# A convolution head that needs only half of its weights to start: one copy on every second partition, the second copy behind

## The chip, the cores and the metric

One core of a Trainium2 chip. The metric is the device time of one execution in microseconds. The kernel before took 275.3 us, the median of 3 runs (274.16 to 279.05).

## What is computed

A 7x7 convolution of a 224x224 image with 96 channels in and out, circular in both directions, written in the reference with FFTs:

```
x: (1, 224, 224, 96) bf16      w: (7, 7, 96, 96) bf16
wp = pad(w, to 224 x 224 in the first two axes)
Xf = rfft2(x over H, W);  Wf = rfft2(wp over H, W)
Yf = einsum('bhwi,hwio->bhwo', Xf, Wf)
y  = irfft2(Yf, (224, 224)).astype(bf16)
```

## The kernel before, in words

**Tiling.** Along H the image is cut into 8 blocks of 28 rows (`NJ`, `B`), and each is transformed with its 6 halo rows by a DFT of length 34: 17 frequencies `s` of two real values. Along W nothing is transformed: the 7 taps are applied directly, two columns at a time. Along W the image is cut into 7 tiles `t` of 32 columns.

**Forward transform.** For each column a matmul of 118 image rows (`xn`, for tile 0 `x0_bufs` at the end of `WF`) by the matrix `Fm` gives the channels on the partitions (`xf`). `f_jobs(t, part)` makes such jobs for a part of the frequencies; `jg` 0 and 1 are the upper and lower four blocks. A job is some 5 to 8 matmuls into one PSUM bank and one cast to `xf`. `jit` then forms sums and differences of `xf` (`J`, called planes here) on VectorE for three frequencies at a time.

**Weights.** `wqx` holds the 49 taps. Before, each tap has two partitions: row 2k holds the tap's 96x96 matrix from its start, row 2k+1 the same from half of the output channels on (`C2` elements later). So one matmul with a strided stationary operand (128 input channels, a step of 96 elements) and the matrix `Em` as the moving one gives two output channels, k and k + 48, for all slots of a group of frequencies. `Em` has a half for the even and a half for the odd rows, with zeros in the others' place. `prep_jobs(gi)` makes 12 jobs of 4 such matmuls for a group of `PGRP`; group 0 is frequencies 0 and 1 (5 slots of 10 taps), the others three frequencies each, for which `diff` forms a third slot per frequency as a difference on VectorE. The results go to `WF`.

**Rounds.** `b_round(t, s)` convolves one frequency of one tile: a first bank, a fill (`mid`), a second bank, a fill (`end`). Fills are jobs of the lists `qs`, with a first and a last fill number each (`add(a, b, jobs)`; round r has fills 2r and 2r + 1), handed out evenly by `pace`. A difference of frequency s must come before round s. Tiles 0 and 1 run interleaved, tile 1 four rounds behind; the others follow one by one.

**Order.** Every engine runs its instructions in program order (`_Ordered`), and so does the queue of transfers on SyncE. Which of VectorE and ScalarE casts a bank is chosen when the program is made, by `evac` with costs of 180 + 1.0n and 160 + 0.85n ns and the running sums `load`.

**The head.** Lines 184 to 190 issue the loads: halo columns, tile 0's pixels of `jg` 0, the weights in two transfers (96 rows, then the last tap's 2 rows), tile 0's pixels of `jg` 1. `warm` (lines 196 to 201) keeps TensorE busy with dummy matmuls on `wu`. Line 222 zeros the end of `wqx`. Lines 683 to 700 are the order of TensorE's work: halo, the forward jobs of `jg` 0, three times nine dummy matmuls, the weights of group 0, the forward jobs of `jg` 1, then tile 1's pixels are requested, planes, rounds.

Of the kernel before, what the change touches and what calls it, by code (L numbers as in the profile page):

```python
# [9 lines left out]
F32 = mybir.dt.float32  # L10
# [15 lines left out]
NB = 8  # L26
POS = TW + HALO
NTAP = 10
TAPS = ((7, 8, 9, 6), (0, 2, 4, 6), (1, 3, 5))
NSLOT = 2 + 3 * (NS - 1)  # L30
PGRP = ((0, 2), (2, 5), (5, 8), (8, 11), (11, 14), (14, 17))
# [16 lines left out]
def slot(s, part):  # L48
    return part if s == 0 else 2 + 3 * (s - 1) + part
# [3 lines left out]
def kernel(  # L53
# [7 lines left out]
    _, H, W, C = x.shape  # L61
# [5 lines left out]
    PW = KT * KT  # L67
    FR = 2 * NS
    PW2 = 2 * PW
    C2 = C // 2  # L70
# [37 lines left out]
    def bank():  # L108
        return pools["psb"].tile([128, 512], F32, name="pb")
# [28 lines left out]
    def dma(out_ap, in_ap):  # L138
        return DE.dma_start(out=out_ap, in_=in_ap)

    WF = cpool.tile([128, NSLOT, NTAP, C], BF16, name="WF")
# [17 lines left out]
    stmp = stmp_cm.__enter__()  # L159
    wqx = wtmp.tile([128, C - 1 + 127 * C + 1], BF16, name="wq")  # L160
    wq = wqx[0:PW2]
    WC = C * C - C2
    Em = wqx[0:PW2, WC:WC + 2 * NSLOT * NTAP].rearrange("p (h a t) -> p h a t", h=2, a=NSLOT)
    XHW = PAD * C + 32
    late = WF[0:R, NSLOT - 8:NSLOT].rearrange("p a t o -> p (a t o)")
    x0_bufs = [late[:, i * (XW + 32):(i + 1) * (XW + 32)] for i in range(2)]
# [14 lines left out]
    def load_x(t, jg):  # L181
        return load_rows(xbuf(t, jg), jg, t * 2 * TW, 2 * TW)
# [2 lines left out]
    for jg in range(2):  # L185
        load_rows(xh_bufs[jg], jg, W - PAD, PAD)
    load_x(0, 0)
    for k, n in ((0, PW - 1), (PW - 1, 1)):
        dma(wqx[2 * k:2 * (k + n), 0:WC], bass.AP(wsrc.tensor, wsrc.offset + k * C * C, [[C * C, n], [C2, 2], [1, WC]]))
    load_x(0, 1)  # L190

    wu = cpool.tile([128, 128], BF16, name="wu")
    wur = wu[:].unsqueeze(1).to_broadcast([128, 4, 128])
# [2 lines left out]
    def warm(n):  # L196
        pwu = bank()
        for _ in range(n):
            TE.matmul(pwu[:].rearrange("p (a b) -> p a b", a=4), lhsT=wu[:, 0:128], rhs=wur, start=True, stop=True)
    warm(8)  # L200
    warm(9)

    ntmp = [0]

# [13 lines left out]
    VE.memset(pi_t[:], math.pi)  # L218
    dmy = ftile([128, 1])
    SE.activation(out=dmy[:], in_=pi_t[:], func=ACTF.Sin, bias=0.0, scale=0.0)  # L220
    zw = wqx[0:PW2, WC + 2 * NSLOT * NTAP:]
    SE.copy(out=zw, in_=wu[0:PW2, 0:1].to_broadcast(list(zw.shape)))

    nrj = ftile([R, JG]); pw_i = ftile([R, 1]); aa = ftile([R, NS, 2]); phf = ftile([R, NS, 2]); phe = ftile([R, NS, 2])
    twc = ftile([PW2, KT]); mf = ftile([R, JG, NS * 2])
# [19 lines left out]
    floor_div(VE, fl[:], qq[:], Q)  # L245
    VE.scalar_tensor_tensor(out=qq[:], in0=fl[:], scalar=-float(Q), in1=qq[:], op0=ALU.mult, op1=ALU.add)
    SE.activation(out=qq[:], in_=qq[:], func=ACTF.Sin, bias=pi_t[:R, :], scale=-2.0 * math.pi / Q)

    GE.memset(mf[:], 1.0)
    GE.affine_select(out=mf[:], in_=mf[:], pattern=[[-B, JG], [0, NS * 2]], compare_op=ALU.is_ge, fill=0.0, base=0, channel_multiplier=1)  # L250
# [26 lines left out]
    VE.tensor_single_scalar(out=pv[:, :, 0], in_=qe[:, 1:, 0], scalar=-2.0, op=ALU.mult)  # L277
    VE.tensor_tensor(out=pv[:, :, 1], in0=qe[:, 1:, 1], in1=qe[:, 1:, 0], op=ALU.subtract)
    VE.tensor_tensor(out=pv[:, :, 2], in0=pv[:, :, 0], in1=pv[:, :, 1], op=ALU.subtract)
    for k0, k1 in ((0, slot(PGRP[0][1], 0)), (slot(PGRP[0][1], 0), NSLOT)):  # L280
        VE.tensor_tensor(out=Em[:, :, k0:k1], in0=pe3[:, k0:k1].unsqueeze(1).unsqueeze(3).to_broadcast([PW2, 2, k1 - k0, NTAP]),
                         in1=mk2[:].unsqueeze(2).to_broadcast([PW2, 2, k1 - k0, NTAP]), op=ALU.mult)

    def build_g(nj):
        PG = nj * FR

        def floor_g(out_ap, in_ap, d):
            GE.tensor_scalar(out=out_ap, in0=in_ap, scalar1=1.0 / d, scalar2=-(d - 1) / (2.0 * d), op0=ALU.mult, op1=ALU.add)
            GE.tensor_single_scalar(out=out_ap, in_=out_ap, scalar=MAGIC, op=ALU.add)
            GE.tensor_single_scalar(out=out_ap, in_=out_ap, scalar=MAGIC, op=ALU.subtract)  # L290

        def mod_g(out_ap, in_ap, fl_ap, d):
            floor_g(fl_ap, in_ap, d)
            GE.tensor_single_scalar(out=out_ap, in_=fl_ap, scalar=-float(d), op=ALU.mult)
            GE.tensor_tensor(out=out_ap, in0=out_ap, in1=in_ap, op=ALU.add)
        p = ftile([PG, 1]); sp = ftile([PG, 1]); rm = ftile([PG, 1]); jp = ftile([PG, 1]); rr = ftile([PG, 1]); z = ftile([PG, 1])
        iota(p[:], [[0, 1]], cm=1)
        mod_g(rm[:], p[:], jp[:], FR)
        mod_g(rr[:], rm[:], sp[:], 2)
        GE.tensor_single_scalar(out=z[:], in_=sp[:], scalar=0.0, op=ALU.is_equal)  # L300
        zr = ftile([PG, 1]); ag = ftile([PG, 1]); pg = ftile([PG, 1]); amp = ftile([PG, 1]); pgt = ftile([PG, 1])
        GE.tensor_tensor(out=zr[:], in0=z[:], in1=rr[:], op=ALU.mult)
        GE.tensor_scalar(out=ag[:], in0=zr[:], scalar1=17.0, scalar2=sp[:, 0:1], op0=ALU.mult, op1=ALU.add)
        GE.tensor_single_scalar(out=ag[:], in_=ag[:], scalar=2.0, op=ALU.mult)
        GE.tensor_tensor(out=pgt[:], in0=rr[:], in1=zr[:], op=ALU.subtract)
        GE.tensor_scalar(out=pg[:], in0=pgt[:], scalar1=17.0, scalar2=17.0, op0=ALU.mult, op1=ALU.add)
        GE.tensor_scalar(out=amp[:], in0=z[:], scalar1=-1.0 / L, scalar2=2.0 / L, op0=ALU.mult, op1=ALU.add)
        nm = ftile([PG, nj, B]); jc = ftile([PG, nj, B]); msk = ftile([PG, nj, B]); fl = ftile([PG, nj, B]); th = ftile([PG, nj, B])
        iota(nm[:], [[0, nj], [1, B]], base=PAD)
        iota(jc[:], [[1, nj], [0, B]])  # L310
        GE.tensor_scalar(out=msk[:], in0=jc[:], scalar1=jp[:, 0:1], scalar2=amp[:, 0:1], op0=ALU.is_equal, op1=ALU.mult)
        GE.tensor_scalar(out=nm[:], in0=nm[:], scalar1=ag[:, 0:1], scalar2=pg[:, 0:1], op0=ALU.mult, op1=ALU.add)
        mod_g(th[:], nm[:], fl[:], Q)

        def fin():
            SE.activation(out=th[:], in_=th[:], func=ACTF.Sin, bias=pi_t[0:PG, :], scale=-2.0 * math.pi / Q)
            GE.tensor_tensor(out=G.rearrange("p (j m) -> p j m", j=nj), in0=th[:], in1=msk[:], op=ALU.mult)
        return fin

    g_fin = build_g(3)  # L320

    def prep_jobs(gi):
        s0, s1 = PGRP[gi]
# [364 lines left out]
    for p in range(2):  # L688
        for f in fj[p][0]:
            f()  # L690
    for _ in range(3):
        warm(9)
    for f in prep_jobs(0)[0]:
        f()
    last = [f() for f in fj[0][1]]
    for jg in range(2):
        for d in load_x(1, jg):
            tc.add_manual_dep(d.ins, last[0].ins.name, SYNC, reason="second tile's pixels later")
    for f in jit(0, 0):
        f()  # L700
    g_fin()
    stmp_cm.__exit__(None, None, None)
    yf_pool = ctx.enter_context(tc.tile_pool(name="yf", bufs=YBUF))
# [21 lines left out]
    def add(a, b, jobs):  # L725
        qs.append([a, b, jobs, len(jobs)])

    for gi in range(1, len(PGRP)):
        pj, dj = prep_jobs(gi)
        add(2 * PGRP[gi - 1][0], 2 * PGRP[gi - 1][1] - 1, pj)  # L730
        for i, f in enumerate(dj):
            k = 2 * (PGRP[gi][0] + i) - 2
            add(k, k + 1, [f])
    for t in range(2):
        scr_tiles[t] = dr_pool.tile([TW, NJ, NS, 4 * C], BF16, name="scr")
# [9 lines left out]
    for r in range(NS + LAG):  # L745
        if r == 0:
            add(0, 4, fj[1][1])
        for p in range(2):
            if r == (1, 3)[p]:
                new_xf(1, SH2[1][p], SH2[1][p + 1])  # L750
                fj = f_jobs(1, p)
                if p == 1:
                    for jg in range(2):
                        fj[jg][-1] = then_load(fj[jg][-1], 2, jg)
                add(2 * r + 1, 2 * r + (5, 8)[p], fj[0] + fj[1])
        for p in range(3):
            if r == (9, 14, 17)[p]:
                new_xf(2, SH2[2][p], SH2[2][p + 1])
                fj = f_jobs(2, p)
                if p == 2:  # L760
                    for jg in range(2):
                        fj[jg][-1] = then_load(fj[jg][-1], 3, jg)
                add(2 * r, 2 * r + (8, 7, 5)[p], fj[0] + fj[1])
        if r == PGRP[-2][1] + 1:
            assert not any(q[2] for q in qs[:4 * len(PGRP) - 8])
            wtmp_cm.__exit__(None, None, None)
            t_pool = ctx.enter_context(tc.tile_pool(name="tt", bufs=NTT, side="right"))
            t2_pool = ctx.enter_context(tc.tile_pool(name="tt2", bufs=1, side="right"))
            yo_pool = ctx.enter_context(tc.tile_pool(name="yo", bufs=2, side="right"))
            g_pool = ctx.enter_context(tc.tile_pool(name="gp", bufs=1, side="right"))  # L770
            GA = g_pool.tile([KA, 4 * B], BF16, name="GA")
            GB = g_pool.tile([128, 2, 4 * B], BF16, name="GB")
            GE.memset(GA[:], 0.0)
            GE.memset(GB[:], 0.0)
        if r == NS + 3:
            queue_c(0)
        for t in range(2):
            s = r - LAG * t
            if not 0 <= s < NS:
                continue  # L780
            now = bursts.pop((r, t), ())
            now = jit(*now) if now else ()
            both = LAG <= r < NS
            b_round(t, s, fills(qs, 2 * r + (t if both else 0)), fills(qs, 2 * r + (t if both else 1)), False, now)
# [116 lines left out]
```

## Time and profile before

| what | value |
|---|---|
| median of 3 runs | 275.3 us |
| span in the profile | 275.8 us |
| TensorE busy | 260.8 us |
| VectorE, ScalarE busy | 227.8, 196.3 us |
| DMA moved | 46.79 MB, mean 170 GB/s |
| granted TensorE clock over the span | 0.993 |
| transfer of the weights (96 rows) | 1719 KB |

How to read it: all instructions go through one helper, so each has line L87, and groups are told apart by the names of their tiles: `pb<-wq` is a weight matmul, `pb<-Fm,xn` or `pb<-Fm,WF` a forward one (tile 0's pixels lie in `WF`), `pb<-WF,xf` and `pb<-WF,J` the convolution, `pb<-wu` a dummy. PE is a matmul, PEld the load of its stationary operand. Times in the stretches and in the timeline are microseconds from the start of the span. In the timeline the first number is the start, the second how long the merged group lasted, and square brackets hold idle time before it and what ended it.

### The profile page before, as it was taken

How to read it: one execution, taken by the hardware profiler on the slowest of the kernel's cores; microseconds unless marked ns; L12 is line 12 of the kernel's file. 1: busy time of each engine (PE TensorE's matmuls, PEld its weight loads, DVE VectorE, ACT ScalarE, POOL GpSimd, SP SyncE). 2: the span in 40 equal slices, each digit the busy share in tenths (PEclk: the TensorE clock that was granted, in tenths of full speed). 3: DMA queues.
4: the chain of work that ended last, by engine and by line, in shares of the span. 5: the costliest groups of instructions: out<-in, count | busy, mean ns of one | idle time of the engine just before them, and what ended most of it. 6: DMA issues, size and time to landing. Idle time of an engine off the chain costs nothing.

```text
span 275.8 us, 12056 instructions
## 1 busy us (share of the span) xinstructions
PE 260.8 (95%) x5088; PEld 238.9 (87%) x5088; DVE 227.8 (83%) x469; ACT 196.3 (71%) x475; POOL 102.2 (37%) x152
## 2 busy tenths in 40 slices
PE   8969999989998999999999999999999999999972
PEld 3649998989998999899999999999999999999751
DVE  5528999998999889977976897788988889899933
ACT  5518997768774566898988869888887874653522
POOL 7720033445446455233243215222432242654200
PEclk9988999999999999999999999999999999999999
DMA  6954313411111189787979487977949833979775
GB/s 176 239 99 128 88 48 108 146 50 48 45 60 67 55 243 191 198 244 230 315 211 256 131 239 222 220 200 200 295 132 180 275 124 110 206 213 241 185 185 181
DMA packets 46211, 46.79 MB, mean 170 GB/s; under 512 B 35274, under 2 KB 37846, under 8 KB 46058
## 3 DMA queue, kind: packets, MB, share of 16 engines
q1 hardware_dynamic: 45692, 44.34, 59.3%
q0 software_dynamic: 464, 1.67, 1.8%
q8 instruction: 40, 0.66, 1.1%
q14 instruction: 15, 0.12, 0.1%
HBM read 24.65 MB, written 21.33 MB: 167 GB/s over the span
## 4 chain that ended last, share of the span: by engine, by line
PE 56%; DVE 17%; DMA 12%; issue 6%; ACT 4%; POOL 3%; SPq 2%; DVEq 0%
PE pb L87 56%; DVE J L87 6%; DMA wq<-in_w_dram 5%; DMA tt<-scr 5%; DVE WF L87 4%; DVE v L87 3%; POOL yf L87 3%; DVE u L87 2%; SPq L87 2%; ACT xf L87 2%; DMA xf<-scrl 2%; ACT WF L87 1%; DVE yf L87 1%; DVE yo L87 0%; DVE xf L87 0%
## 5 line engine op out<-in xcount | busy, mean ns | idle before, releaser
L87 PE MATMUL pb<-WF,J 96*128 96x96 bf16 x2898 | 167.6, 206 | 1.4 <-DVE J L87 0.6
L87 PEld LDWEIGHTS <-J 96*128 96x128 bf16 x2898 | 141.5, 98 | 10.7 <-DVE J L87 1.7
L87 POOL TENSOR_TENSOR yf<-v,u 128x384 bf16<-128x384 f32 x85 | 85.2, 1018 | 141.7 <-issue 84.8
L87 ACT CAST xf<-pb 96x408 bf16<-96x408 f32 (+5 forms) x142 | 66.9, 492 | 7.8 <-PE pb L87 5.8
L87 PE MATMUL pb<-WF,xf 96*128 96x96 bf16 x952 | 61.0, 206 | 2.9 <-DVE WF L87 2.1
L87 DVE TENSOR_TENSOR J<-xf 96x1824 bf16<-96x1824 bf16 (+1 forms) x84 | 60.3, 756 | 0.1
L87 PEld LDWEIGHTS <-xf 96*128 96x128 bf16 x952 | 47.4, 98 | 3.8 <-issue 3.1
L87 PE MATMUL pb<-Fm,xn 118*128 118x136 bf16 (+4 forms) x576 | 44.5, 203 | 0.0
L87 ACT CAST WF<-pb 96x480 bf16<-96x480 f32 (+1 forms) x60 | 30.0, 561 | 8.4 <-PE pb L87 8.1
L87 PE MATMUL pb<-tt,Gm 102*84 102x384 bf16 (+1 forms) x132 | 33.6, 327 | 0.0
L87 PEld LDWEIGHTS <-xn 118*128 118x128 bf16 x576 | 29.2, 98 | 0.1
L87 ACT CAST yo<-pb 84x384 bf16<-84x384 f32 (+1 forms) x61 | 26.3, 480 | 4.1 <-PE pb L87 4.0
L87 ACT CAST J<-pb 84x384 bf16<-84x384 f32 (+1 forms) x62 | 26.8, 482 | 2.7 <-PE pb L87 2.7
L87 DVE TENSOR_TENSOR J<-J 96x912 bf16<-96x912 bf16 (+1 forms) x42 | 24.9, 594 | 0.0
L87 PE MATMUL pb<-wq 98*128 98x120 bf16 (+1 forms) x288 | 22.9, 234 | 2.1 <-DMA wq<-in_w_dram 2.1
L87 PEld LDWEIGHTS <-wq 98*128 98x128 bf16 x288 | 20.5, 151 | 2.5 <-issue 2.5
L87 PE MATMUL pb<-wu 128*128 128x512 bf16 (+3 forms) x70 | 18.7, 398 | 1.1 <-DVE ct L87 1.1
L87 DVE TENSOR_TENSOR yf<-v,u 128x384 bf16<-128x384 f32 x27 | 15.6, 578 | 0.9
L87 DVE TENSOR_TENSOR WF<-WF 96x960 bf16<-96x960 bf16 x15 | 15.8, 1057 | 0.2
L87 PEld LDWEIGHTS <-wu 128*128 128x128 bf16 (+3 forms) x70 | 7.9, 115 | 8.4 <-issue 2.9
L87 DVE CAST WF<-pb 96x400 bf16<-96x400 f32 (+1 forms) x12 | 7.2, 608 | 8.4 <-PE pb L87 8.1
L87 PEld LDWEIGHTS <-Gm 102*84 102x84 bf16 (+1 forms) x132 | 11.5, 117 | 1.7 <-issue 0.6
(394 smaller groups left out, 236.9 us busy)
## 6 DMA issues: line engine op xcount, KB each, us to landing
scr<-yf SPq DMA_DIRECT2D x30, 288.0 KB
xn<-in_x_dram SPq DMA_DIRECT2D x12, 672.0 KB
tt<-scr SPq DMA_DIRECT2D x24, 336.0 KB
out_dram<-yo SPq DMA_DIRECT2D x12, 252.0 KB
out_dram<-J SPq DMA_DIRECT2D x12, 252.0 KB
tt<-scr SPq DMA_DIRECT2D x6, 288.0 KB
wq<-in_w_dram SPq DMA_DIRECT2D x1, 1719.0 KB
scrl<-yf POOLq DMA_DIRECT2D x5, 288.0 KB, 5.1
```

What stands on the lines that cost most here:

```text
L87: r = fn(*a, **k)
```

## The change

The head is to start on half the weight bytes. The first copy of the weights (even rows, whole 96x96 matrices) is loaded alone, in three pieces by columns; the odd rows are zero meanwhile, since a matmul reads all of them. ScalarE writes the zeros, over all 96 rows, each third ahead of its piece. Frequencies 0 and 1 then come from that copy by 96 matmuls with one output channel each (`first_prep`), in 12 jobs of 8, of which 6 stand ahead of the forward jobs of `jg` 1 and 6 behind. The second copy (odd rows) follows when these matmuls are done, ahead of group 1. The last tap's row is loaded in 16 pieces. The matrix `Em` moves behind the full first copy, and VectorE zeros the end of `wqx`. Tile 1's pixels are requested at once instead of after the forward jobs. Group 1's weight jobs move from fills 0 to 2 to fills 2 and 3, its first difference from fill 2 to 3, and tile 1's first forward jobs from fills 3 to 6 to fills 0 to 2. Dummy matmuls: 9 and 11 in place of 8 and 9 at the start, twice 5 in place of three times 9 later. The bound of the assertion on finished lists changes with the lists.

```diff
-    WC = C * C - C2
-    Em = wqx[0:PW2, WC:WC + 2 * NSLOT * NTAP].rearrange("p (h a t) -> p h a t", h=2, a=NSLOT)
+    WA = C * C
+    WC = WA - C2
+    WZ = WA // 3
+    Em = wqx[0:PW2, WA:WA + 2 * NSLOT * NTAP].rearrange("p (h a t) -> p h a t", h=2, a=NSLOT)
...
-    for k, n in ((0, PW - 1), (PW - 1, 1)):
-        dma(wqx[2 * k:2 * (k + n), 0:WC], bass.AP(wsrc.tensor, wsrc.offset + k * C * C, [[C * C, n], [C2, 2], [1, WC]]))
-    load_x(0, 1)
+
+    def load_w(h, cuts):
+        for a, b in zip(cuts[:-1], cuts[1:]):
+            dma(wqx[h:2 * PW - 3 + h:2, a:b], wsrc[0:PW - 1, h * C2 + a:h * C2 + b])
+
+    def load_wl(h, n):
+        dma(wqx[2 * PW - 2 + h:2 * PW - 1 + h, 0:n].rearrange("p (a b) -> p a b", a=16), wsrc[PW - 1:PW, h * C2:h * C2 + n].rearrange("p (a b) -> p a b", a=16))
+    load_wl(0, WA)
...
-    warm(8)
     warm(9)
+    warm(11)
...
-    zw = wqx[0:PW2, WC + 2 * NSLOT * NTAP:]
-    SE.copy(out=zw, in_=wu[0:PW2, 0:1].to_broadcast(list(zw.shape)))
+    zw = wqx[0:PW2, WA + 2 * NSLOT * NTAP:]
+
+    def zero(eng, ap):
+        o = ap.bitcast(F32)
+        z = wu[0:ap.shape[0], 0:2].bitcast(F32).to_broadcast(list(o.shape))
+        return eng.copy(out=o, in_=z) if eng is SE else eng.tensor_copy(out=o, in_=z)
+    zero(SE, wqx[0:PW2 - 2, 0:WZ])
...
     SE.activation(out=qq[:], in_=qq[:], func=ACTF.Sin, bias=pi_t[:R, :], scale=-2.0 * math.pi / Q)
+    for i in range(1, 3):
+        zero(SE, wqx[0:PW2 - 2, i * WZ:(i + 1) * WZ])
+    load_w(0, (0, WZ, 2 * WZ, WA))
+    load_x(0, 1)
+    for jg in range(2):
+        load_x(1, jg)
...
+    zero(VE, zw)
...
+    def first_prep():
+        n = slot(PGRP[0][1], 0)
+        q = n * NTAP
+        wv = WF[0:C, 0:n].rearrange("i a t o -> i (a t) o")
+
+        def mk_(o0):
+            def f():
+                pw = bank()
+                pv_ = pw[:, 0:NB * q].rearrange("p (k q) -> p k q", q=q)
+                for k in range(NB):
+                    o = o0 + k
+                    TE.matmul(pv_[:, k], lhsT=wqx[0:PW2 - 1, o:o + 127 * C + 1:C], rhs=Em[0:PW2 - 1, 0, 0:n].rearrange("p a t -> p (a t)"), start=True, stop=True)
+                apart(("W", 0), o0, evac(wv[..., o0:o0 + NB], pv_[0:C].rearrange("i k q -> i q k"), NB * q))
+            return f
+        return [mk_(o0) for o0 in range(0, C, NB)]
...
-    for _ in range(3):
-        warm(9)
-    for f in prep_jobs(0)[0]:
+    for _ in range(2):
+        warm(5)
+    pj = first_prep()
+    for f in pj[:6]:
         f()
-    last = [f() for f in fj[0][1]]
-    for jg in range(2):
-        for d in load_x(1, jg):
-            tc.add_manual_dep(d.ins, last[0].ins.name, SYNC, reason="second tile's pixels later")
+    for f in fj[0][1]:
+        f()
+    for f in pj[6:9]:
+        f()
     for f in jit(0, 0):
         f()
+    for f in pj[9:]:
+        f()
+    load_w(1, (0, WC))
+    load_wl(1, WC)
     g_fin()
...
-        add(2 * PGRP[gi - 1][0], 2 * PGRP[gi - 1][1] - 1, pj)
+        add(*((2, 4) if gi == 1 else (2 * PGRP[gi - 1][0], 2 * PGRP[gi - 1][1] - 1)), pj)
         for i, f in enumerate(dj):
-            k = 2 * (PGRP[gi][0] + i) - 2
+            k = 2 * (PGRP[gi][0] + i) - (1 if gi == 1 and i == 0 else 2)
...
-            if r == (1, 3)[p]:
+            if r == (0, 3)[p]:
...
-                add(2 * r + 1, 2 * r + (5, 8)[p], fj[0] + fj[1])
+                add(2 * r + p, 2 * r + (3, 8)[p], fj[0] + fj[1])
...
-            assert not any(q[2] for q in qs[:4 * len(PGRP) - 8])
+            assert not any(q[2] for q in qs if q[1] <= 2 * r)
```

## The prediction

> **What bounds the kernel now.** I read the page's engine table and slices first, then the stretches of the head, then its timeline, then who waited for whom on TensorE.
>
> ```profile
> PE 260.8 (95%) x5088; PEld 238.9 (87%) x5088; DVE 227.8 (83%) x469; ACT 196.3 (71%) x475; POOL 102.2 (37%) x152
> ```
>
> TensorE is busy for 95% of the span, and from 24 us on it has few waits of any length (0.3 us at most between 24 and 40 us), so a microsecond won ahead of the first round goes to the end, unless a later wait takes it back. The head is where TensorE does no useful work. The stretches (us; busy time of PE, PEld, DVE, ACT, POOL; then granted clock, DMA share, GB/s) and the timeline show why:
>
> ```profile
> 10.40:14.20 3.80, 3.80 (x23) 1.74 (x20) 0.84 (x2) 1.06 (x3) 3.11 (x13) 1.00 1.00 214
> 14.20:18.40 4.20, 2.17 (x11) 0.78 (x8) 0.00 (x0) 0.00 (x0) 1.67 (x5) 1.00 0.79 141
> 18.40:22.60 4.20, 4.15 (x55) 4.18 (x56) 2.96 (x6) 2.81 (x6) 0.00 (x0) 0.59 0.03 12
> ```
> ```profile
> 10.38 3.84 PE L87 MATMUL pb<-wu 128*128 128x512 bf16 x17
> 12.76 3.62 PE L87 MATMUL pb<-wu 128*128 128x512 bf16 x16
> 18.45 3.99 PE L87 MATMUL pb<-wq 98*128 98x100 bf16 x48 [2.08 <-DMA wq<-in_w_dram]
> 22.24 1.27 PE L87 MATMUL pb<-Fm,WF 118*128 118x64 bf16 x32
> 23.97 0.51 PE L87 MATMUL pb<-WF,xf 96*128 96x96 bf16 x8 [0.46 <-ACT xf L87]
> 24.32 1.16 PE L87 MATMUL pb<-wq 98*128 98x120 bf16 x16
> 31.69 0.33 PE L87 MATMUL pb<-WF,xf 96*128 96x96 bf16 x4 [0.24 <-DVE WF L87]
> ```
>
> From 10.4 to 18.45 us TensorE does only dummy matmuls (wu) and waits for the weights (wq). Then 48 weight matmuls, the late forward jobs of tile 0, and at 23.97 the first convolution. DMA is full to about 14 us. The chain of waits names the transfer that ends last:
>
> ```profile
> 3.87 14.44 DMA wq<-in_w_dram
> ```
>
> That is not the 96-row transfer but the second one, two rows of 18,336 bytes: in the trace's semaphore records the 96 rows arrived at 13.8 to 16.8 us, the two rows at 17.3 and 18.3.
>
> [...] two arrivals against sixteen. [...] after the 2.08 us wait the granted clock is 0.59 between 18.4 and 22.6. [...] and I price a byte the same; no row of before shows a stepped transfer.
>
> **The change part by part.**
>
> Zeros. One 1.94 us copy becomes three copies of 1536 fp32 elements[...]. The first stands where the old one was (2.2 to 3.7); the sine at 4.05 stays; the others end at 7.4. They hide: ScalarE was idle to 7.31. VectorE's zeros (1036 fp32) are unseen before: [...] at most 1.26 by the rate of the 98x900 product (1095 ns). I take 1.2. About 0.7 falls into VectorE's wait before that product, the rest delays the first casts by 0.5 us, ahead of dummy matmuls. Cost nothing.
>
> First copy. SyncE issues each third of it after the zeros below it: 3.8, 6.0, 7.4 us. Ahead of it go the halo columns and tile 0's first pixels, which is what DMA moved by 8 us anyway (1.21 MB had ended by 8.0, 0.22 of it weights). Of the new 0.885 MB, 0.67 is left at 8.0; at 240 KB/us (the slice at 6 to 10.5 us has 249) that is 2.8 us: 10.8, with 1.2 for the slowest engine and the arrival, **12.0** in place of 18.3. The last tap's row is now in 16 pieces and early.
>
> TensorE to the first round. Forward jobs end at 10.4 as before; 10 dummy matmuls at 0.215 (17 took 3.84) to 12.55, so the weights are there and the clock stays full. The 96 new matmuls: the spacing of wq matmuls in the 16 that took 1.16 us is (1.16 - 0.22)/15 = 63 ns at 120 columns, and starts in the trace are 64 apart at 100 columns before the clock falls. It doesn't follow the columns[...]. So halving the columns to 50 saves nothing: 96 x 64 = 6.1 us. Order: 48 (3.07) to 15.6, 32 forward matmuls (0.95) to 16.6, 24 (1.54) to 18.1, 24 to 19.7; last cast 0.7 more: the first convolution at **20.4**, against 23.97. Tile 0's second pixels (0.72 MB behind the weights) arrive about 14.5 to 15, just in time. The planes, 2.05 us of VectorE after those casts, end near 20.5 and are needed at about 22. **Gain 3.5 us.**
>
> Second copy. It overwrites zeros that all 96 matmuls read, so SyncE holds it until the last of them, at 19.9. Ahead of it stand tile 1's pixels (1.45 MB), ending near 20. Time to arrival: tile 1's first half, 0.69 MB, was issued at 23.45 and was in at 28.66, 5.2 us; 16 KB/us for each engine gives 0.9 more for 0.9 MB. Low end 4.5 (the 18 KB rows at 1.28 us, three to an engine, plus start); high end 7.5 (behind late pixels, at 204 GB/s as between 8 and 19.5 us). I take 5.7: **25.6**.
>
> Round 0. Fills are now two and one late forward jobs of tile 0 and six early jobs of tile 1, no weight jobs. TensorE: 22 convolution matmuls of 43 ns, 17 of 32 ns and 48 of 29 ns, 2.9 us; then the first bank of round 1, 0.8: it asks for the second copy at 24.2. **Wait 1.4 us.** Behind it on TensorE stands everything, nothing else can go.
>
> Round 1. All twelve jobs of the second weight group (before: eight of them in rounds 0 and early 1) now fall into round 1, six in each half, with five forward jobs. TensorE needs 4.6 us: 48 x 64 ns, 42 forward matmuls, 14 convolutions. The casts: VectorE gets five, then v (0.54) and the planes (2.05); by the costs in `evac` the six of the second half all go to ScalarE, 11 x 0.5 us in all, ending 6.3 us after the copy is in. Then the difference (0.65) for round 2's third part. So that convolution starts at 25.6 + 6.9 = 32.5, and TensorE stood for 2.0 us of it, less 0.3 that it stood before: **1.7 us lost**. Check against before: there it started at 31.69, with six forward jobs fewer done, 48 x 29 ns = 1.4 us: 33.1, so 0.6 ahead.
>
> Sum: -3.5 + 1.4 + 1.7 = -0.4; the check says -0.6. I take -0.5. Later rounds do the same work in total; the six jobs come off rounds 1 to 3.
>
> **Rivals.** *The gain stays:* the copy is in by about 24.2 (low end), and ScalarE isn't six casts behind, since casts spread more evenly than I count. Then -3.5 + 0 + 1.0 = -2.5, 272.8 us. For: DMA has nothing else to do after 20; my cast split is by hand. Against: five waits of TensorE on VectorE's WF, 2.4 us up to 120 us, show that this edge already binds. *Slower:* tile 1's pixels are late, the copy arrives at 27.4 (+1.8), and the wait halves the clock for 3.4 us as before, about +0.6 on the weight matmuls (83 against 64 ns) and +0.6 on the rest: -0.5 + 3.0 = +2.5, 277.8 us. For: a wait of 2.08 us did so before, and DMA ran at 214 GB/s and less when it had to serve all queues' tails. Against: the rows are smaller (6 KB) until the second copy.
>
> **How the numbers follow.** Forecast 0.5, gain stays 0.3, slower 0.2. Time: 275.3 - 0.5 = 274.8. Range: from 272.3, beyond the first rival, to 277.4, most of the second. Over 2% is 5.5 us either way, more than either rival; only an unseen size gives that: 0.05 faster, 0.05 slower, 0.90 the same.
>
> **What would show each step.** The first wq matmul near 12.6 at full clock; 64 ns between them; the first convolution (WF, xf) near 20.4; then a TensorE wait for DMA wq near 24 of 1 to 2 us; then waits on WF casts and the difference just before round 2. The forecast is wrong if wq isn't waited for at all, or if the first convolution starts after 22 us.

## The result: slower by 3.7%, and the profile after

The changed kernel takes 285.6 us (284.89 to 286.68), the kernel before beside it 276.9 us (274.16 to 279.05): a ratio of 1.037, with a 95% interval of 1.029 to 1.045. The forecast was 274.8, no change.

The engine table and the row of granted clocks of the kernel after:

```profile
PE 267.4 (94%) x5122; PEld 245.1 (86%) x5122; DVE 228.4 (80%) x468; ACT 200.3 (70%) x479; POOL 102.2 (36%) x152
...
PEclk9975979999999999999999999999999999999967
```

TensorE is busy 6.6 us longer for 34 instructions more. That isn't work (48 weight matmuls more and 14 dummies fewer, some 3 us each): the slices show a lower clock in the head (9975979, seven slices of 7.1 us) and in the last two. The mean clock is 0.961, against 0.993.

The stretches of the head, in the windows of the prediction (length; then busy time of PE, PEld, DVE, ACT, POOL; then clock, DMA share, GB/s):

```profile
10.40:14.20 3.80, 3.48 (x33) 1.70 (x29) 0.69 (x2) 1.79 (x5) 3.22 (x11) 1.00 1.03 267
14.20:18.40 4.20, 2.78 (x46) 2.78 (x47) 4.17 (x9) 0.97 (x2) 2.37 (x4) 0.86 1.02 291
18.40:22.60 4.20, 4.20 (x78) 4.20 (x77) 4.06 (x8) 2.77 (x6) 0.00 (x0) 0.50 0.30 83
22.60:28.00 5.40, 4.82 (x86) 4.73 (x85) 2.09 (x5) 4.47 (x11) 0.36 (x1) 0.55 0.65 163
```

DMA is now full to 18.4 us, as wanted. But VectorE, nearly idle to 14.2, is full right after, and the clock is at half from 18.4 on. In the clock's own records it is at half from 17.21 to 27.45 us, from 37.69 to 41.11, and from 273.21 to 280.04: three windows of 3.41 us, one, and two. (A last one starts at 283.45, with TensorE's work done.)

The timeline of the head, with SyncE's transfers, ScalarE's and VectorE's zeros, and TensorE (start, how long the group lasted, what it did; in brackets the idle time before it and what ended it):

```profile
3.11 5.93 SPq L87 DMA_DIRECT2D wq<-in_w_dram  x4
4.30 2.83 ACT L87 COPY wq<-wu 96x1536 f32<-96x1536 f32 x2
11.79 2.32 PE L87 MATMUL pb<-wu 128*128 128x512 bf16 x10
13.51 0.70 DVE L87 COPY wq<-wu 98x1036 f32<-98x1036 f32 x1 [7.99 <-DMA wq<-in_w_dram]
14.12 1.44 DVE L87 TENSOR_TENSOR wq<-ct,ct 98x100 bf16<-98x100 f32 x2
15.48 3.13 DVE L87 CAST xf<-pb 96x408 bf16<-96x408 f32 x6
15.62 3.11 PE L87 MATMUL pb<-wq 97*128 97x50 bf16 x48 [1.52 <-DVE wq L87]
18.55 1.88 PE L87 MATMUL pb<-Fm,WF 118*128 118x64 bf16 x32
20.25 3.05 PE L87 MATMUL pb<-wq 97*128 97x50 bf16 x48
23.87 0.80 PE L87 MATMUL pb<-WF,xf 96*128 96x96 bf16 x8 [0.58 <-DVE J L87]
29.89 1.67 PE L87 MATMUL pb<-wq 98*128 98x120 bf16 x24 [0.53 <-DMA wq<-in_w_dram]
36.16 0.33 PE L87 MATMUL pb<-WF,J 96*128 96x96 bf16 x4 [1.54 <-ACT WF L87]
37.34 0.33 PE L87 MATMUL pb<-WF,xf 96*128 96x96 bf16 x4 [0.68 <-DVE WF L87]
```

The first weight matmul is not at 12.55 but at 15.62, and what it waited for is not the weights but VectorE. VectorE wrote its zeros (0.70 us) after a wait of 7.99 us for the first copy of the weights, then `Em`, without which no weight matmul can go. So the first convolution starts at 23.87, 0.1 us ahead of before (23.97), and the price of the second copy is paid with nothing won.

The chain of work that ended last (start, how long, what), in part, has the other delay:

```profile
4.39 2.74 ACT wq L87 x2
...
7.15 0.63 SPq L87
...
7.82 0.58 SPq L87
...
8.45 4.98 DMA wq<-in_w_dram
...
13.51 0.06 DVE wq L87
```

All three thirds of the copy were issued behind the last of ScalarE's zeros, at 7.15, 7.82 and 8.45 us, not one by one from 3.8 on. The last was in at 13.43. (The last tap's row is not in 16 pieces on the chip, as the section on the change has it: the trace has it as one packet of 18,432 bytes. It was early, in at 7.26 us, since it was issued first.)

Neither wait is needed by the data. VectorE's zeros lie from column 10,216 on and `Em` from 9,216 on, the copy ends at column 9,216; and the first third touches only the columns of the first zeros. The instructions as they were built, VectorE's zeros and the first third, carry the waits, on three DMA queues and on ScalarE:

```
L87 TensorCopy wq<-wu 98x1036 [waits DMAHW7_49,DMAHW1_49,DMAHW0_49]
L87 DMACopy wq<-in_w_dram 48x3072 [waits Activation_49]
```

The program's ordering of writes to one tile takes each stepped transfer as touching the columns of its neighbours too. (That the step of the partitions is the reason is inferred, not shown by a run: before, `Em` was written at 6.33 us while the 96-row transfer into the same tile was in flight.)

How far behind the first profile of before the kernel is, at the end of a round's sums: 0.41 us in round 0, 0.65 in round 1, 4.7 in round 2, 6.26 in round 4 (at 50 us). From there it is constant, 5.9 to 6.4 but for two single sums, to 260 us. In the last 12 us 3.8 are added up to TensorE's last stage; the output behind it gives one back, so that the whole span is 9.2 us longer.

### The profile page after: what moved, and what is told of

It is laid out like the page before. It is cut to its first block, busy times and chain, and to the rows that moved or that the text cites. A ratio compares the mean times of both kernels' runs of the same rounds, so it can differ in the third digit from the quotient of the medians.

```text
span 284.9 us, 12134 instructions
## 1 busy us (share of the span) xinstructions
PE 267.4 (94%) x5122; PEld 245.1 (86%) x5122; DVE 228.4 (80%) x468; ACT 200.3 (70%) x479; POOL 102.2 (36%) x152
## 4 chain that ended last, share of the span: by engine, by line
PE 54%; DVE 21%; issue 8%; DMA 7%; POOL 4%; ACT 3%; SPq 1%; DVEq 0%; POOLq 0%; ACTq 0%
PE pb L87 54%; DVE J L87 8%; DVE WF L87 4%; DMA wq<-in_w_dram 4%; DVE v L87 4%; POOL yf L87 4%; DMA tt<-scr 2%; DVE u L87 2%; DVE yf L87 1%; DMA xf<-scrl 1%; ACT wq L87 1%; ACT WF L87 1%; SPq L87 1%; DVE ct L87 1%; DVE yo L87 1%
## 5 line engine op out<-in xcount | busy, mean ns | idle before, releaser
L87 ACT CAST yo<-pb 84x384 bf16<-84x384 f32 (+1 forms) x61 | 26.3, 480 | 3.8 <-PE pb L87 3.7
L87 PE MATMUL pb<-wq 98*128 98x120 bf16 (+1 forms) x336 | 25.6, 232 | 2.0 <-DVE wq L87 1.5
L87 PEld LDWEIGHTS <-wq 98*128 98x128 bf16 (+1 forms) x336 | 23.2, 153 | 2.7 <-DVE wq L87 2.0
L87 PE MATMUL pb<-wu 128*128 128x512 bf16 (+3 forms) x56 | 16.4, 417 | 1.1 <-DVE ct L87 1.1
L87 DVE TENSOR_TENSOR WF<-WF 96x960 bf16<-96x960 bf16 x15 | 17.0, 1133 | 0.5 <-ACT WF L87 0.5
L87 PEld LDWEIGHTS <-wu 128*128 128x128 bf16 (+3 forms) x56 | 6.8, 122 | 7.5 <-issue 3.8
L87 DVE CAST tt<-pb 112x384 bf16<-112x384 f32 x8 | 4.4, 556 | 8.5 <-PE pb L87 8.3
```

The costliest lines, as they stand in the source:

```text
L87: r = fn(*a, **k)
```

## The experiments

**The two waits, alone and together.** Theory A: `Em` and VectorE's zeros ahead of it are held back by a wait that the data doesn't need. Theory B: the second loss, behind round 1, belongs to the second copy and stays when A is mended. `declare_no_dep` tells the ordering that two writes don't meet; the columns are disjoint, so no race comes with it.

VectorE's wait alone (e1), with the same call around both writes of `Em`:

```diff
+    wd = []
+
+    def beside(r, ds):
+        for d in ds:
+            tc.declare_no_dep(r.ins, d.ins, reason="disjoint columns of wq")
+        return r
...
-            dma(wqx[h:2 * PW - 3 + h:2, a:b], wsrc[0:PW - 1, h * C2 + a:h * C2 + b])
+            wd.append(dma(wqx[h:2 * PW - 3 + h:2, a:b], wsrc[0:PW - 1, h * C2 + a:h * C2 + b]))
...
-    zero(VE, zw)
+    beside(zero(VE, zw), wd)
```

> The changed kernel with one thing undone: VectorE's three writes to the end of wq (the zeros and the two products for Em) no longer wait for the three transfers of the first copy, whose columns they don't touch. Theory A (this wait is what made the change slow: 8.0 us of VectorE, which delays the weight matmuls to 15.6 us and lets the clock fall to half for 10.2 us): first weight matmul at about 13.5, when the first copy is in, clock full, first convolution near 21.3, second copy in near 27, total 276 to 278 us against 285.6. Theory B (round 1 is what costs: the second copy, twelve weight jobs in one round and the difference behind them): at most 3 us come back, total 282 to 285.

Both (e2): e1, and each third waits only for the zeros below it. Later the thirds alone (i3), which is e2 without `beside` on VectorE's three writes:

```diff
-        zero(SE, wqx[0:PW2 - 2, i * WZ:(i + 1) * WZ])
+        zs.append(zero(SE, wqx[0:PW2 - 2, i * WZ:(i + 1) * WZ]))
...
+    for i in range(3):
+        beside(wd[i], zs[i + 1:])
```

> As the run before, and each third of the first copy waits only for the zeros below it, not for all three. Theory A: thirds issued at about 3.8, 6.0 and 7.2 us in place of 7.15, 7.8 and 8.45, first copy in near 12.0, first weight matmul at 12.6, first convolution at 20.4 as forecast, 0.9 us less than the run before: 275 to 277 us. Theory B: no difference to the run before within 1 us, since round 1 waits for the second copy either way.

> The changed kernel with the other wait undone alone: each third of the first copy waits only for the zeros below it; VectorE's zeros and Em still wait for all three thirds. The copy is in near 12.0 in place of 13.4, so VectorE is released 1.4 us earlier, first weight matmul at 14.1 to 14.2. If each wait costs its own delay: 1.4 us back, 284.0, about as e1_no_dve_wait (283.9). If the clock decides: the dummy matmuls end at 14.1 since the late casts hold TensorE up, there is hardly a gap, the clock stays full and 3 us or more come back, 282 or less.

| kernel | us, median (range) | ratio to before | first weight matmul, first convolution | behind before at 50 to 260 us |
|---|---|---|---|---|
| after | 285.6 (284.89 to 286.68) | 1.037 [1.029, 1.045] | 15.62, 23.87 | 5.9 to 6.4 |
| e1, without VectorE's wait | 283.88 (283.16 to 285.1) | 1.030 [1.026, 1.035] | 14.07, 22.52 | 4.3 to 4.8 |
| i3, without the thirds' wait | 283.28 (281.34 to 284.51) | 1.024 [1.017, 1.031] | 14.07, 22.26 | 3.9 to 4.4 |
| e2, without both | 279.33 (278.96 to 280.2) | 1.014 [1.010, 1.018] | 12.11, 19.54 | 1.8 to 2.3 |

The timeline of e2:

```profile
3.10 4.65 SPq L87 DMA_DIRECT2D wq<-in_w_dram  x4
12.11 3.04 PE L87 MATMUL pb<-wq 97*128 97x50 bf16 x48
14.99 1.09 PE L87 MATMUL pb<-Fm,WF 118*128 118x64 bf16 x32
15.92 3.05 PE L87 MATMUL pb<-wq 97*128 97x50 bf16 x48
19.54 0.50 PE L87 MATMUL pb<-WF,xf 96*128 96x96 bf16 x8 [0.58 <-ACT WF L87]
25.37 1.70 PE L87 MATMUL pb<-wq 98*128 98x120 bf16 x24 [1.96 <-DMA wq<-in_w_dram]
28.77 2.85 ACT L87 CAST WF<-pb 96x480 bf16<-96x480 f32 x6 [0.31 <-PE pb L87]
31.67 0.48 PE L87 MATMUL pb<-WF,J 96*128 96x96 bf16 x4 [1.54 <-ACT WF L87]
32.85 0.48 PE L87 MATMUL pb<-WF,xf 96*128 96x96 bf16 x4 [0.38 <-DVE WF L87]
```

This is the head that the prediction described: the weights at 12.1, the first convolution at 19.5, the wait for the second copy (1.96 us), six casts of 0.475 us in a row on ScalarE, the waits behind them. The numbers that were expected came out wrong, though: e1 lies where B had it (282 to 285), not A (276 to 278), and e2 lies outside both (275 to 277, or within 1 us of e1). VectorE's wait alone is the smaller part. For both waits together A holds: they are worth 6.3 us by the medians, 1.037 against 1.014 by the ratios. Through the first convolution they don't add: alone 1.35 and 1.61 us, together 4.33. Either wait alone still holds the first weight matmul to 14.07, and in e1 and i3 the clock is at half for 10.24 us of the head (from 15.74 and 16.95), in e2's profile not at all. From the first weight matmul to the first convolution it takes 8.45, 8.19 and 7.43 us in e1, i3 and e2, so up to 1.0 of the 4.33 is the clock. Part of the 4.33 comes back at the second copy's wait (0.53 us in after, 1.96 in e2), so that from 50 us on it is 1.6, 2.0 and 4.1. The rest is in the last 12 us, below. B holds too: e2 has the waits of the second copy and is still 1.4% slower than before.

**The clock.** Theory C: the wait of 1.52 us lets the clock fall to half in the head; more dummies would hold it (e3).

```diff
     for _ in range(2):
-        warm(5)
+        warm(9)
```

> The changed kernel, waits and all, with twice 9 dummy matmuls in place of twice 5, so that TensorE is busy until the first weight matmul at 15.6 us and its clock stays full. This prices the clock alone. Theory A, with the wait as the main cost: first weight matmul unchanged at 15.6, first convolution near 23.0 in place of 23.9, then a longer wait for the second copy; 1 to 2 us back, total 283.5 to 284.5. If the halved clock is the main cost: 4 us or more back, total under 282.

283.23 us (282.98 to 284.28), ratio 1.028 [1.024, 1.032]. The clock fell all the same, at 18.73 for 10.24 us, and the first convolution was at 23.75. But e3 doesn't settle C, since the dummies left a wait:

```profile
15.72 3.06 PE L87 MATMUL pb<-wq 97*128 97x50 bf16 x48 [0.82 <-DVE wq L87]
```

i3 does: there TensorE has no wait ahead of the first weight matmul, so C as stated falls. Its line and stretches:

```profile
14.07 3.02 PE L87 MATMUL pb<-wq 97*128 97x50 bf16 x48
```

```profile
14.10:16.90 2.80, 2.80 (x48) 2.80 (x49) 2.80 (x6) 0.98 (x2) 2.12 (x6) 1.00 1.02 271
16.90:27.10 10.20, 9.62 (x163) 9.53 (x162) 6.71 (x13) 7.41 (x17) 0.36 (x1) 0.50 0.41 111
```

TensorE is busy for every nanosecond that the profile shows (2.80 of 2.80), and then the clock is at half for 10 us in which it is busy for 94%. Theory D: a stretch with nothing but matmuls of 50 columns, one every 60 to 64 ns, counts as little work (a dummy of 512 columns takes 0.215 us in before, so 50 columns are some 21 ns by estimate), and a wait is only another way to little work. For a test, in e2 the same 96 matmuls with both halves of `Em`, 100 columns, the second result written over by the next matmul (h2; what is kept is the same):

```diff
-                    TE.matmul(pv_[:, k], lhsT=wqx[0:PW2 - 1, o:o + 127 * C + 1:C], rhs=Em[0:PW2 - 1, 0, 0:n].rearrange("p a t -> p (a t)"), start=True, stop=True)
+                    TE.matmul(pw[:, k * q:(k + 2) * q].rearrange("p (h q) -> p h q", h=2), lhsT=wqx[0:PW2 - 1, o:o + 127 * C + 1:C],
+                              rhs=Em[0:PW2 - 1, :, 0:n].rearrange("p h a t -> p h (a t)"), start=True, stop=True)
```

> On e2_thirds, each of the 96 first weight matmuls has 100 columns in place of 50 (both halves of Em; the second half is zeros and its columns are written over by the next matmul). By the spacing of 64 ns, which doesn't follow the columns, this costs no time. Theory D (50 columns in 64 ns keep the array busy for a third of the time, and a clock window filled by these matmuls counts as idle, which is why f2_clock_kept and f5_second_in_thirds fell to half at 16.1 and 19.7 with no wait in sight): no half clock in the window over the first weight matmuls, times spread less, median 0.5 to 1 us below e2_thirds. If only waits halve the clock: no change.

279.37 us (279.02 to 281.13), ratio 1.013 [1.007, 1.020], not the 0.5 to 1 us less of D, and the clock as in e2, which hadn't fallen in the head either: nothing on D. It does show that the columns are free: the 96 matmuls with the forward jobs between them take from 12.11 to 18.88 us, with 50 columns to 18.74. f2 tried to hold the clock in e2 behind the head, with dummies ahead of group 1's first job and at the end of round 1:

```diff
+            pj[0] = lambda f=pj[0]: (warm(9), f())
...
+            add(3, 4, [lambda: warm(8)])
```

> On e2_thirds, 9 dummy matmuls ahead of the first weight job of group 1 (in the 1.96 us wait for the second copy) and 8 at the end of round 1 (in the 1.54 us wait for casts). Nothing else moves, the waits stay. Theory C (clock): no half clock between 31 and 39 us, 1.5 us or more back, 277.8 or less; the shift against the kernel before at the fifth sum of tile 0 falls from 2.2 to about 0.6. Theory A (the waits alone cost): no change, or slower by what the dummies overrun.

280.42 us (277.44 to 282.76), ratio 1.012 [1.005, 1.018]. In its profile the clock fell at 16.09, in the head that it shares with e2, for 10.24 us, again with TensorE busy throughout; between 26.3 and 272 us it was full. That profile is of the longest of its four executions, so it says little on its own question.

**Columns per window.** The traces together decide D as far as counting can. The clock changes only in steps of 3.41 us: each stay at one level that a trace holds whole is a multiple of it. So each trace can be cut into such windows from the place of its first fall, and in each the columns of all matmuls that start there can be added up (a dummy has 512, a first weight matmul 50). From 3.4 us on, the 17 profiles have 1,290 such windows at full clock:

| columns in the window | windows | followed by half clock |
|---|---|---|
| under 3,500 | 21 | 21 |
| 3,500 to 4,130 | 20 | 4 |
| over 4,130 | 1,249 | 0 |

Busy time does not sort them: i3's window from 13.54 us has TensorE busy for 97% and 2,976 columns, and the clock falls; h0's from 266.26 has 55% and 3,840, and it stays. In after, the window over the wait of 1.52 us has 1,300 columns. In e2 the two windows over the head have 4,098 each and the clock stays; f2 has the same head, but its windows lie otherwise, one has 3,594, and the clock falls. i2, with 100 columns, has 5,744 and 5,504 there. By this count narrow matmuls and waits do the same thing, and which execution is hit depends on where its windows lie. It is a count over kernels that differ in much else; no run changed the columns alone in a head where the clock had fallen.

**How early the copy of before was.** Was it the last tap's row, as the prediction read, that held the head of before? b1 writes the load of that row as 16 pieces and leaves all else of the kernel before:

```diff
-    for k, n in ((0, PW - 1), (PW - 1, 1)):
-        dma(wqx[2 * k:2 * (k + n), 0:WC], bass.AP(wsrc.tensor, wsrc.offset + k * C * C, [[C * C, n], [C2, 2], [1, WC]]))
+    dma(wqx[0:2 * (PW - 1), 0:WC], bass.AP(wsrc.tensor, wsrc.offset, [[C * C, PW - 1], [C2, 2], [1, WC]]))
+    for h in range(2):
+        dma(wqx[2 * PW - 2 + h:2 * PW - 1 + h, 0:WC].rearrange("p (a b) -> p a b", a=16), wsrc[PW - 1:PW, h * C2:h * C2 + WC].rearrange("p (a b) -> p a b", a=16))
```

> The kernel before with one part of the change alone: the last tap's two rows are loaded in 16 pieces each. All weights in near 16.9 in place of 18.3 us, so the first convolution 1.4 us earlier or more, since the idle time shrinks to 0.5 us and the clock may stay full (the 48 weight matmuls then take 3.1 in place of 4.0 us): 273 to 274.5 us against 275.3 to 276.9. If the 96-row transfer is as late as the small one: no difference.

276.79 us (275.12 to 279.05), ratio 1.004 [1.001, 1.006]; the first weight matmul at 18.0 instead of 18.45. That is no answer, since the transfer didn't become what the edit says: in the trace each of the two rows is still one packet of 18,336 bytes with one arrival, at 16.81 and 17.96 us. The 96 rows were in at 17.10, so the last tap's row still held the first weight matmul. The kernel before, once more and unchanged (h0), has the other case:

> The kernel before, unchanged, for a second profile. Its times spread over 274 to 280.5 us, and the first profile, 277.5, lies above their median. If the clock windows make the spread, this profile has other ones than the first (which had 3.4 us at half from 19.2 and 2.6 at the end), with the same work between: sums of tile 0 and 1 shifted by at most 2 us as one block.

276.79 us (274.96 to 280.32), ratio 1.001 [0.998, 1.004]. But the profile is of an execution of 275.04 us, where that of before was of one of 277.49, and in its timeline the head reads otherwise:

```profile
17.08 3.21 PE L87 MATMUL pb<-wq 98*128 98x100 bf16 x48 [0.83 <-DMA wq<-in_w_dram]
...
21.68 0.51 PE L87 MATMUL pb<-WF,xf 96*128 96x96 bf16 x8 [0.46 <-ACT xf L87]
```

The weights came 1.4 us sooner, the clock stayed full, and the first convolution is at 21.68, not 23.97. Here the two rows were in at 16.26 and 16.59 and the 96 rows last, at 17.04 (before: 17.3, 18.3 and 16.8). So the prediction's reading, that the two rows end last, is right for one execution and not for the other, and with both early the copy would still be as late as about 17. The 2.2 us between the two profiles go unchanged to 260 us. So the gain to be had in the head is between 2.1 us (e2 against this one) and 4.4 (e2 against the first), by execution. With nine more dummies ahead of the weights in the kernel before (i1):

```diff
-    for _ in range(3):
+    for _ in range(4):
         warm(9)
```

> The kernel before with 36 dummy matmuls in place of 27 ahead of the first weight matmul, so that TensorE is busy until the weights are in. Theory C (in part of its runs the wait for the weights halves the clock for 3.4 us, as in its first profile but not in its second): head as in the second profile in all runs, median about 0.5 to 1 us lower and fewer runs above 278. If its spread comes from elsewhere (the arrival of transfers, the end): no change.

275.97 us (275.07 to 277.2), ratio 0.998 [0.995, 1.001]; the first weight matmul at 18.28 without a wait, the first convolution at 22.83, the clock 0.999. Its executions spread over 2.1 us, those of before beside it over 4.8 (4.0 without the three longest). That fits a clock that falls in the head in some executions of before; the time is not told from that of before.

**What is left of e2.** All of these start from e2. Does the second copy come sooner in three pieces of columns (f5)?

```diff
-    load_w(1, (0, WC))
+    load_w(1, (0, WC // 3, 2 * WC // 3, WC))
```

> On e2_thirds, the second copy is loaded in three pieces of 6,112 bytes a row in place of one of 18,336. If the rate of a transfer depends on the length of its rows (before: 1.28 us for a packet of 18,336 bytes, 0.345 for one of 6,144, so 14.3 and 17.8 KB/us on each engine): in 0.6 to 0.8 us earlier than the 6.4 us after its issue, and as much back at the end, 278.6. If the 6.4 us are a matter of bytes and latency alone: no change.

280.42 us (279.07 to 282.9), ratio 1.016 [1.011, 1.022]. It was used 6.2 us after its issue, against 6.4 in e2: no gain. Can the forward jobs of round 1 go ahead of the weight jobs, to fill the wait (f4)? Group 1's jobs then join the lists behind tile 1's forward jobs of round 0.

```diff
+        if gi == 1:
+            first_group = add_group
+        else:
+            add_group()
...
+        if r == 0:
+            first_group()
```

> On e2_thirds, in fill 2 the four forward jobs stand ahead of the six weight jobs of group 1 in place of behind them. Theory A: TensorE has 1.1 us of work while the second copy is still on its way, the wait for it falls from 1.96 to about 0.9 and the end of round 1 comes 1 us earlier: 278.3. Theory C: the shorter wait may also keep the clock; then 2 us or more. If the casts of round 1 bound it and not TensorE: less than 0.5 us.

280.4 us (278.82 to 282.71), ratio 1.016 [1.010, 1.022]. The wait for the copy fell from 1.96 to 1.22 us, but those ahead of round 2 stayed (1.52 and 0.57), and from 50 us on it is under 0.5 us ahead of e2: what binds round 1 is not TensorE's wait but, it seems, the casts. VectorE leaves ScalarE those casts because it has the planes to form. So f1 forms the planes of frequencies 3 to 5 of tile 0 a round later, and h1 a round earlier (a minus where f1 has a plus):

```diff
-            bursts[(g0 - 2, 1 if g0 - 2 >= LAG else 0)] = (0, g)
+            bursts[(g0 - 2 + (g == 1), 1 if g0 - 2 >= LAG else 0)] = (0, g)
```

> On the kernel of e2_thirds (both waits of the first copy undone; 279.3 us), the planes of tile 0's frequencies 3 to 5 are formed in round 2 in place of round 1. Theory A (what is left is round 1: VectorE's 2.05 us of planes send all six late casts to ScalarE, and TensorE stands 1.54 + 0.38 us ahead of round 2): the two waits shrink to under 0.8 us together, 1 us or more back, 278.3 or less. Theory C (what is left is the halved clock from 31.6 to 38.5, which the wait for the second copy alone brings about): no more than 0.3 us back.

> On e2_thirds, the planes of tile 0's frequencies 3 to 5 are formed in round 0, where VectorE stands (22.3 to 25.4 us there), in place of round 1. Theory A (round 1's casts bind): the planner then gives some late casts to VectorE, the difference starts about 5.3 us after the second copy is in, in place of 6.3, the wait ahead of round 2 falls from 1.54 + 0.38 to under 0.8 us, and no wait for planes comes in round 3 as with f1_planes_later: 1.2 us or more back against e2_thirds with the same clock. If round 1 is bound by TensorE: less than 0.5 us.

f1: 279.84 us (278.6 to 282.57), ratio 1.014 [1.009, 1.020]. Ahead of round 2 only 0.61 us is left, but there is a new wait, as the table of who waited for whom has it:

```profile
PE pb L87 <- DVE J L87: 1.9, 1, 1.9
PE pb L87 <- DMA wq<-in_w_dram: 1.8, 1, 1.8
```

The planes came too late for round 3. h1: 277.87 us (275.12 to 279.51), ratio 1.004 [1.001, 1.007]. Ahead of round 2 it too waits 0.62 us:

```profile
31.92 0.33 PE L87 MATMUL pb<-WF,J 96*128 96x96 bf16 x4 [0.62 <-ACT WF L87]
```

It has no wait for planes in round 3; a wait of 1.24 us for VectorE comes up at 43.2. Against h2, which takes as long as e2 and ran beside it, h1 takes 1.5 us less (its profile is of an execution of 279.32). How much of that is the casts is not shown, because the clock has a part in it. In e2 it is at half from 31.62 to 38.45, behind the waits of round 1; in f1 and h1 it is full there (h1 has one window at half earlier, from 25.25). And f1, whose four longest waits between 19 and 45 us add up to 4.9 us against 4.5 in e2, is from 50 us on 2.6 us ahead of e2 and 0.5 ahead of the first profile of before, like h1 (0.3); it loses that in the last 12 us. So shorter waits ahead of round 2 gain in two ways, by themselves and by the clock behind them.

Together (h3): e2 with the edits of h1, f4 and h2. And with few dummies in f2's two places (i2):

```diff
+                pj[0] = lambda f=pj[0]: (warm(4), f())
...
+            add(3, 4, [lambda: warm(3)])
```

> e2_thirds with planes in round 0, forward jobs ahead of weight jobs in fill 2, and 100 columns in the first weight matmuls. If theories A and D hold, the gains add: wait for the second copy 1.2 us, wait ahead of round 2 under 0.8, clock full in the head: sums of tile 0 from the fifth on about 2 us earlier than in the first profile of before, 274 to 276 us, level with or below the kernel before. If they don't: 279 as e2_thirds.

> h3_combined with 4 dummy matmuls in its 1.0 us wait for the second copy and 3 in the 0.9 us wait ahead of round 2. Theory C: no half clock at 31.5 (3.4 us there), 0.8 us back, 277.0, level with the kernel before (276.7). If the window falls for another reason, for instance because matmuls at 64 ns spacing count as half idle: no change, or slower by what the dummies overrun.

h3: 277.79 us (275.63 to 279.04), ratio 1.005 [1.002, 1.007], where 274 to 276 was expected. i2: 276.25 us (275.4 to 278.39), ratio 0.999 [0.996, 1.003], level with before. The dummies did keep the clock, which in h3 is at half from 31.5 to 34.9 us and in i2 full. But between 50 and 260 us the two are the same (0.7 to 1.2 us ahead of the first profile of before, 1.0 to 1.5 behind the second), so nothing was won there. Where their profiles differ, by 1.7 us up to TensorE's last stage, is the last 12 us.

**The end of the span.** This is open in part. In after, the last forward stage waits 2.74 us for pixels from `scrl` (1.92 in the first profile of before, 1.53 in the second), the clock falls at 273.21, and 3.8 us are lost. The stretch of after:

```profile
273.00:280.00 7.00, 6.27 (x20) 4.36 (x21) 3.34 (x6) 2.39 (x5) 0.00 (x0) 0.52 0.47 148
```

The clock is at half at this place also in the profiles of e1, i3, f1, f2, h1 and h3 (waits of 1.9 to 2.7 us), not in e2, e3, f5, h2 and i2 (1.5 to 2.2), nor in f4, which waits 2.53. The columns sort these too: the window that the wait falls into has 2,304 in after and 1,536 to 3,072 in the other six, and at least 3,840 where the clock stays, because the wait is shorter or lies over two windows. Why the wait is longer was not found, and no run changed it alone.

## Why the prediction was wrong, by its steps

**Zeros: "Cost nothing."** The step that failed. The durations were right or better (ScalarE's first third from 2.20 for 1.45 us, VectorE 0.70; the author's estimates were 2.2 to 3.7 and 1.2 us). Their waits weren't asked for. VectorE's zeros stood 7.99 us behind the copy, and behind them on the same engine `Em` and its first casts. So ScalarE alone cast the forward jobs, and they ended at 11.8 us, not 10.4.

**First copy: "issues each third of it after the zeros below it: 3.8, 6.0, 7.4 us."** Failed in the same way: 7.15, 7.82 and 8.45. With both waits gone (e2) issues are at 3.68, 5.87 and 7.25, the weights are used at 12.11 (forecast 12.55) and the first convolution is at 19.54 (forecast 20.4). That a byte costs the same in rows on every second partition was the author's estimate, and so was the 1.2 us for the slowest engine and the arrival; in after, with such rows in flight up to 13.43, DMA moved 267 GB/s from 10.4 to 14.2 us. These two steps account for 4.1 us at 50 us and for 6.3 of the median; the 2.2 between the two figures lie in the last 12 us, where the longer wait is unexplained. What e2 is still slower than before (1.4%, 3.6 us) is not theirs; it belongs to the steps below.

**"Gain 3.5 us."** The reference was mis-sized: 23.97 was one execution with the clock at half. Against 21.68 e2's head gains 2.1 us. That the last tap's row is "now in 16 pieces" is wrong for the trace (one packet); that it is early is right.

**TensorE's order and the 64 ns.** Right: 48 matmuls in 3.04 to 3.11 us with 50 columns, also with the clock at half; 3.10 to 3.17 with 100, at full clock. What sets the 64 ns was not tested. In before the load of a strided `wq` operand takes 151 ns and that of `xf` or `J` 98, and convolution matmuls of 96 columns start every 43 ns. That "the clock stays full" came true in e2 with some luck: its windows over the head have 4,098 columns each, and those of the same head in f2, which lie otherwise, let it fall.

**Second copy: "Wait 1.4 us", "1.7 us lost".** Right in kind, a little low. It took 6.4 us from issue to use where 5.7 was taken, inside the bounds 4.5 to 7.5; e2 waits 1.96 us. (The 16 KB/us for each engine was an estimate; in before a packet of 18,336 bytes takes 1.277 us in the median, 14.4 KB/us, and one of 6,144 takes 0.353 between 20 and 30 us, 17.4 KB/us.) The six casts on ScalarE and the difference were as counted by hand: the third part of round 2 at 32.85 (forecast 32.5), with 1.54 and 0.38 us of waits ahead of it.

**The rivals.** "Slower" had the fall of the clock, taken from one window of before (3.41 us at 0.50 from 19.19, after the wait of 2.08 us), but only one such window, for 1.2 us. There were four windows in or near the head and two at the end, and not for the wait that it named. In e2 the clock falls too, behind the waits for casts ahead of round 2 (31.62 to 38.45 us), and e2 goes from 0.49 us behind before to 2.17 in rounds 2 to 4. "The gain stays" fails even in e2: the copy is late and the casts of round 1 bind TensorE for 1.54 us, and the clock behind them adds to it; f4, f1 and h1 don't part the two.

The prediction's own test, the first convolution after 22 us, was the right one: it was at 23.87. With the waits mended, the change is still not faster. What the head wins by half a copy, round 1 and the clock behind it give back, since all twelve weight jobs of group 1 then stand where casts and planes already fill two engines.

## What to carry to other kernels

Before a new write into a shared tile is priced at nothing, ask what the program makes it wait for, not only what it must wait for: here writes of under 1.5 us each, with no element in common with the transfers that they held up or waited for, cost 4.1 us of 285.6 at 50 us, and 6.3 by the medians, through the order that they were given. Read the head from two executions before you count a gain in it, since its clock and its arrivals moved by 2.2 us here. And work that is moved behind a later arrival lands in a round; look first which engine's casts that round has room for.

## What the runs showed of the hardware that was not expected

The granted clock did not follow the profile's busy time. In i3 it fell to 0.50 after 2.8 us in which TensorE is busy throughout, with 48 matmuls of 50 columns in 3.02 us, and stayed there for three windows of 3.41 us. Counted in columns it is regular over the 17 profiles: all 21 windows with under 3,500 were followed by half clock, none of the 1,249 with over 4,130.

A weight matmul, whose stationary operand is strided by 96 elements, starts every 60 to 65 ns at full clock (median 60 with 50 columns in after, 64 with 100 and 63 with 120 in before): 100 columns in place of 50 cost 0.14 us over the 96 matmuls of h2. At half clock 50 columns still take about 60 ns (after), 100 take 83 (before) and 120 take 100 (after).

The second copy, 48 rows on every second partition and 0.9 MB, is used 6.2 to 6.6 us after its issue where TensorE waits for it, in rows of 18 KB (e2 6.4, after 6.6) and in thirds of them (f5 6.2) alike.
